# Pipelined evictions in the second network, with its splits, its operands and its conversion moved

## The chip, the cores and the metric

The kernel runs on one core of a Trainium2 chip. The metric is the device time of one execution in microseconds, the median of several runs. TensorE (PE in the rows) does the matrix products, VectorE (DVE), ScalarE (ACT) and GpSimd (POOL) the elementwise work; SyncE (SP) issues the DMAs. Every engine takes its instructions in the order in which the program lists them, and an instruction that waits holds up those behind it on its engine.

## The reference, cut to what matters

```python
attn = softmax over a window of 64 positions of (q @ k.T) / sqrt(64)   # 2 x 8 heads, 576 positions
x = (attn @ v), as 1152 tokens x 512
out = 0
for e in range(4):                      # mixture: w1 512 x 1024, w2 1024 x 512
    h = np.maximum(x @ w1[e], 0.0)
    out += p[:, e:e + 1] * (h @ w2[e])
h = out @ w_in                          # second network: w_in 512 x 2048, w_out 2048 x 512
g = np.maximum(h, 0.0) + alpha * np.minimum(h, 0.0)
return g @ w_out
```

`w_in` and `w_out` arrive as 64-bit floats, everything else as 32-bit floats.

## The kernel before

Attention runs first, interleaved with stage 0 of the mixture. From then on the work goes in stages of 512 hidden columns: stages 1 to 7 are the rest of the mixture, stages 8 to 11 the second network (`S1 = 8`, `NST = 12`). Tokens are in two parts, p = 0 with 512 tokens and p = 1 with 640.

A stage has two phases. Phase A computes the hidden values with one level of a seven-product scheme over 2x2 blocks, which needs sums of blocks of x and w as operands. For each part there are seven units A(s, p, i), i = 0 to 6, and each does one product for u = 0 and one for u = 1, of 256 columns (p = 0) or 320 (p = 1). Products 0, 1 and 2 are copied out of PSUM by ACT (`keep`, L401). Products 3 to 6 end one result each: DVE adds PSUM and the kept copy (`total`, L405; product 6 needs none) and `evict` does the rest. Phase B, nine units B(s, p, t), multiplies the hidden values with w2, and DVE adds each result to `acc` (L523, L527; in stage 8 ACT copies it, L525). A product is done with a high and a low part of each operand, so each operand is split: ACT rounds to the high part, DVE or POOL subtracts to get the low one. The splits are `forms_w1` (L166) for w1 and its block sums, `split_w2` (L210) for w2, `x_first` and `x_second` (L346, L352) for x and its block sums.

In the second network `evict` (L432) has four steps for a result. ACT makes `g` = relu(-src) (L438); DVE makes g = g * alpha + src (L439); `flush(1)` then issues, for the result before this one, ACT's high part `hh` (L484) and POOL's low part `hl` (L485). In the mixture there is one ACT and one DVE instruction for a result.

Between stage 7 and stage 8 the operand x changes: the sums in `acc` are transposed on PE (`x2_unit`, L534), copied by ACT to `raw`, and split. Part 0 of it is split during B(7, 1), part 1 during A(8, 0) and B(8, 0), which run before A(8, 1). B(8, 0) takes its units in the order 2, 3, 0, 1.

The 64-bit weights are converted to 32-bit by integer steps on the device: 32 tiles (`conv_steps`, L228), five steps for a tile: ACT L248 and L249; DVE L251 and L252; DVE L255 and the load of a later tile; DVE L260; DVE L263 with POOL L264 and L265. Then a DMA writes the tile to scratch memory (L267). The tile `ct` has six slots of 512 values in a buffer of 3072: a, two of r, two of y and e; y of tile n + 2 takes the slot that the DMA of tile n reads. `pace` (L691) says how many steps follow each unit: 18 in a mixture stage from stage 2 on (four in A, 14 in B), and in the second network two after each B unit and four in A. `load_w` first issues all steps that its tile still lacks (`convert`, L138).

Other work is given to units by `plan`; a list for each unit is issued after its products. A load of weights is issued after the unit in which the buffer that it takes was used last. PSUM has eight banks, taken in turn.

## Time and profile before

| | us |
|---|---|
| median of 3 runs | 688.3 (687.38 to 689.62) |
| the profiled execution, whole | 687.76 |
| its span, first to last instruction | 685.9 |
| PE busy | 624.6 (91% of the span) |
| DVE busy | 459.9 (67%) |
| ACT busy | 315.0 (46%) |
| POOL busy | 286.0 (42%) |

PE's busy time counts every matmul at the length it had, also where the clock was halved. The share of an engine over the whole span says little here, because the stages differ; the stage boundaries can be read from PE's timeline, where L394 is phase A and L504 phase B.

### The profile page before, as it was taken

The numbers are of one execution on the slowest core, as the hardware profiler recorded it, in microseconds if no ns is written. First come the engines' busy times: TensorE is split into PE (matmuls) and PEld (weight loads), VectorE is DVE, ScalarE is ACT, GpSimd is POOL, SyncE is SP. The second block draws the span as 40 slices with busy tenths as digits, with TensorE's granted clock in tenths as the row PEclk, the third lists the DMA queues.
The fourth block names the chain that finished last, engine by engine and source line by source line (L and its number), as shares of the span: only waits on it lengthen the run. The fifth ranks groups of instructions, "written<-read, shape, count | busy, mean of one in ns | idle before, by whom it ended". The sixth has DMA issues, their size and how long they took to land. (4 is left out here: it accounts for less than half of the span.)

```text
span 685.9 us, 10878 instructions
## 1 busy us (share of the span) xinstructions
PE 624.6 (91%) x4032; PEld 555.0 (81%) x4032; DVE 459.9 (67%) x962; ACT 315.0 (46%) x783; POOL 286.0 (42%) x310
## 2 busy tenths in 40 slices
PE   4799989999999999999999999969798972899898
PEld 3678778989989889899898898858687852888886
DVE  4756659676786877867878666862476588566452
ACT  4555435535426426336155263654465522542640
POOL 4636744053143341450524315444553664464340
PEclk9999999999999999999999999979999995899999
DMA  9742001251241251341322420310041125001012
GB/s 320 257 148 63 2 0 63 96 166 62 92 154 63 93 168 45 129 135 62 138 93 85 151 74 15 123 63 0 1 125 60 62 100 207 16 21 57 1 48 92
DMA packets 31653, 62.59 MB, mean 91 GB/s; under 512 B 2288, under 2 KB 11760, under 8 KB 30576
## 3 DMA queue, kind: packets, MB, share of 16 engines
q1 hardware_dynamic: 31600, 61.90, 26.4%
q8 instruction: 31, 0.51, 0.3%
q14 instruction: 22, 0.18, 0.1%
HBM read 51.14 MB, written 10.75 MB: 90 GB/s over the span
## 5 line engine op out<-in xcount | busy, mean ns | idle before, releaser
L504 PE MATMUL o<-w2l,hh 128*128 128x512 f32 (+1 forms) x400 | 156.9, 392 | 7.1 <-ACT hh L484 7.1
L504 PE MATMUL o<-w2h,hl 128*128 128x512 f32 (+1 forms) x400 | 156.4, 391 | 0.1
L504 PE MATMUL o<-w2h,hh 128*128 128x512 f32 (+1 forms) x400 | 156.1, 390 | 0.0
L264 POOL TENSOR_TENSOR ct<-ct 128x512 f32<-128x512 f32 x32 | 44.9, 1402 | 154.7 <-DVE ct L260 85.5
L504 PEld LDWEIGHTS o<-w2l,hh 128*128 128x128 f32 x400 | 75.9, 190 | 22.7 <-ACT hh L484 7.9
L504 PEld LDWEIGHTS o<-w2h,hl 128*128 128x128 f32 x400 | 75.7, 189 | 16.7 <-POOL hl L485 1.2
L504 PEld LDWEIGHTS o<-w2h,hh 128*128 128x128 f32 x400 | 75.9, 190 | 15.0
L485 POOL TENSOR_TENSOR hl<-g,hh 128x256 fp32r<-128x256 f32 (+1 forms) x64 | 52.9, 833 | 68.0 <-ACT hh L484 67.0
L394 PE MATMUL X<-xth,wfl 128*128 128x256 f32 (+1 forms) x264 | 60.2, 310 | 21.3 <-ACT s L401 12.7
L201 DVE TENSOR_TENSOR w2l<-ws,w2h 128x512 fp32r<-128x512 f32 x48 | 36.2, 753 | 50.2 <-ACT w2h L200 50.0
L394 PEld LDWEIGHTS X<-xth,wfl 128*128 128x128 f32 x264 | 43.3, 195 | 25.7 <-ACT s L401 13.8
L523 DVE SCALAR_TENSOR_TENSOR acc<-o,pn,acc 128x512 f32<-128x512 f32 x63 | 46.6, 745 | 21.7 <-PE o L504 21.6
L188 POOL TENSOR_TENSOR sr<-ws 128x256 f32<-128x256 f32 x42 | 38.3, 911 | 52.4 <-DVE wfl L197 44.7
L394 PE MATMUL X<-xtl,wfh 128*128 128x256 f32 (+1 forms) x264 | 57.7, 301 | 0.0
L394 PE MATMUL X<-xth,wfh 128*128 128x256 f32 (+1 forms) x264 | 57.5, 300 | 0.0
L265 POOL TENSOR_TENSOR ct<-ct 128x512 f32<-128x512 f32 x32 | 42.5, 1328 | 33.1 <-DVE ct L263 31.8
L196 ACT ACTIVATE wfh<-sr 128x1024 fp32r<-128x1024 f32 x22 | 23.3, 1059 | 64.2 <-POOL sr L188 62.0
L248 ACT ACTIVATE ct<-wd 128x512 f32<-128x512 uint32 x32 | 21.3, 666 | 66.9 <-DMA cv<-ct 56.5
L394 PE MATMUL Z<-xth,wfl 128*128 128x320 f32 (+1 forms) x176 | 38.7, 301 | 9.2 <-DVE acc L527 9.2
L394 PEld LDWEIGHTS X<-xtl,wfh 128*128 128x128 f32 x264 | 43.8, 195 | 0.0
L394 PEld LDWEIGHTS X<-xth,wfh 128*128 128x128 f32 x264 | 43.6, 194 | 0.0
L197 DVE TENSOR_TENSOR wfl<-sr,wfh 128x1024 fp32r<-128x1024 f32 x22 | 26.9, 1221 | 21.9 <-ACT wfh L196 21.8
(152 smaller groups left out, 1382.2 us busy)
## 6 DMA issues: line engine op xcount, KB each, us to landing
ws<-in_moe_w_dram SPq DMA_DIRECT2D x16, 1024.0 KB, 5.5
wd<-in_moe_w_in_dram SPq DMA_DIRECT2D x16, 512.0 KB, 3.7
cv<-ct SPq DMA_DIRECT2D x32, 256.0 KB, 2.4
wd<-in_moe_w_out_dram SPq DMA_DIRECT2D x16, 512.0 KB, 3.6
ws<-cv SPq DMA_DIRECT2D x8, 1024.0 KB, 5.0
v<-in_v_dram SPq DMA_DIRECT2D x16, 256.0 KB, 5.7
q<-in_q_dram SPq DMA_DIRECT2D x6, 384.0 KB, 6.8
out_dram<-acc SPq DMA_DIRECT2D x8, 256.0 KB, 2.0
```

The costliest lines, as they stand in the source:

```text
L188: e.tensor_tensor(out=sr[o // 2][:, o % 2], in0=x, in1=y, op=op)
L196: nc.scalar.activation(out=view(hi), in_=src, func=AF.Copy)
L197: nc.vector.tensor_tensor(out=view(lo), in0=src, in1=view(hi).bitcast(F32), op=ALU.subtract)
L201: nc.vector.tensor_tensor(out=lv, in0=src, in1=hv.bitcast(F32), op=ALU.subtract)
L248: nc.scalar.activation(out=y, in_=low, func=AF.Copy, scale=2.0 ** -52)
L264: nc.gpsimd.tensor_tensor(out=y, in0=y, in1=e, op=ALU.mult)
L265: nc.gpsimd.tensor_tensor(out=y, in0=r, in1=y, op=ALU.add)
L394: nc.tensor.matmul(ps, lhsT=w[:, d, :], rhs=x[:, d, :], start=(first and m == 0), stop=(m == 5), skip_group_check=True)
L485: nc.gpsimd.tensor_tensor(out=hl, in0=gg, in1=hh.bitcast(F32), op=ALU.subtract)
L504: nc.tensor.matmul(ps, lhsT=h_t[s, p, f][a][:, t * P:(t + 1) * P], rhs=w_t[2, s, f][b][:, cols], start=(n == 0), stop=(n == 3 * NF - 1))
L523: nc.vector.scalar_tensor_tensor(out=at, in0=ps, scalar=sc, in1=at, op0=ALU.mult, op1=ALU.add)
```

## The change

- Evictions of the second network (s >= 8). `evict` now only issues ACT's relu, into a tile `r`, and puts the result in a queue `heads`. `activate` is called after every product: it issues DVE's L439 step of the results in `heads` but the last one, and ACT's and POOL's `hh` and `hl` for the results in a second queue, `tails`, down to a given number that stay: up to four in stages 9 to 11 (they are issued at the next products 0 and 1, or at the first two B units), up to one in stage 8, none from product 5 on. g overwrites the `total` tile, except for product 6, whose g goes to `r`.
- `split_w2` in the second network: at units (0,0), (0,1), (1,0), (1,1) rather than (0,2), (0,5), (1,1), (1,4); in stage 8 at (0,0) twice, (0,1), (0,2). The load of w2 for the stage after moves with the last of them.
- Changeover operands of part 1: forms 1 and 2 are added on POOL at A(8,0,2) and A(8,0,3), forms 3 and 4 on DVE at B(8,0,2) and B(8,0,3), and all splits (ACT and DVE or POOL) go to B(8,0). Before, adding and splitting stood at A(8,0,2) to B(8,0,1), adding on DVE, low parts on POOL.
- Conversion: `ct` has seven slots, three of them for y; a mixture stage issues 22 steps from stage 2 on (18 in B), stage 8 five, and stages 9 and 10 fewer in B and at i = 1, 2 in A.

```diff
-    xr1 = sb.tile([P, 3072], F32, tag="big", name="xr1")
+    xr1 = sb.tile([P, 3584], F32, tag="big", name="xr1")
...
-            a, r, y, e = [view(ct[:, o]) for o in (0, 1 + n % 2, 3 + n % 2, 5)]
+            a, r, y, e = [view(ct[:, o]) for o in (0, 1 + n % 2, 4 + n % 3, 3)]
...
-            nc.sync.dma_start(out=conv[which, s][:, f, :], in_=ct[:, 3 + n % 2])
+            nc.sync.dma_start(out=conv[which, s][:, f, :], in_=ct[:, 4 + n % 3])
...
-    def x_second(p, raw, f, o, w, add_engine, lo_engine):
+    def x_second(p, raw, f, o, w, add_engine, lo_engine, keep=0):
...
-        nc.scalar.activation(out=hi, in_=src, func=AF.Copy)
-        lo_engine.tensor_tensor(out=lo, in0=src, in1=hi.bitcast(F32), op=ALU.subtract)
+        splits.append((hi, lo, src, lo_engine))
+        while len(splits) > keep:
+            split_next()
...
+    def split_next():
+        if splits:
+            hi, lo, src, e = splits.pop(0)
+            nc.scalar.activation(out=hi, in_=src, func=AF.Copy)
+            e.tensor_tensor(out=lo, in0=src, in1=hi.bitcast(F32), op=ALU.subtract)
...
-            evict(s, p, 2 * u + 1, 0, ps)
+            evict(s, p, 2 * u + 1, 0, ps, True)
             del sets[s, p, u]
-        low_parts(1)
+        if s >= S1:
+            activate(1 if i > 2 else 0, int(i < 5) if s == S1 else (2, 0, 4)[min(i, 2)])
+        else:
+            low_parts(1)
...
-            g = late["mid"].tile([P, HALF[1]], F32, tag="g", bufs=3, name=f"g{s}_{p}_{f}_{half}")[:, 0:HALF[p]]
-            nc.scalar.activation(out=g, in_=src, func=AF.Relu, scale=-1.0)
-            nc.vector.scalar_tensor_tensor(out=g, in0=g, scalar=alph[:, col:col + 1], in1=src,
-                                           op0=ALU.mult, op1=ALU.add)
-            tails.append((hh, hl, g))
-            flush(1)
+            r = late["mid"].tile([P, HALF[1]], F32, tag="r", bufs=3, name=f"r{s}_{p}_{f}_{half}")[:, 0:HALF[p]]
+            nc.scalar.activation(out=r, in_=src, func=AF.Relu, scale=-1.0)
+            heads.append((hh, hl, r, alph[:, col:col + 1], src, r if direct else src))
...
-    def flush(keep):
-        while len(tails) > keep:
-            hh, hl, gg = tails.pop(0)
-            nc.scalar.activation(out=hh, in_=gg, func=AF.Copy)
-            nc.gpsimd.tensor_tensor(out=hl, in0=gg, in1=hh.bitcast(F32), op=ALU.subtract)
+    def activate(keep, later):
+        while len(heads) > keep:
+            hh, hl, r, col, src, g = heads.pop(0)
+            nc.vector.scalar_tensor_tensor(out=g, in0=r, scalar=col, in1=src, op0=ALU.mult, op1=ALU.add)
+            tails.append((hh, hl, g))
+        while len(tails) > later:
+            hh, hl, g = tails.pop(0)
+            nc.scalar.activation(out=hh, in_=g, func=AF.Copy)
+            nc.gpsimd.tensor_tensor(out=hl, in0=g, in1=hh.bitcast(F32), op=ALU.subtract)
...
-            units = [(0, i) for i in range(NF)] if s == S1 else [(0, 2), (0, 5), (1, 1), (1, 4)]
+            units = [(0, 2), (0, 5), (1, 1), (1, 4)] if s < S1 else [(0, 0), (0, 1), (1, 0), (1, 1)]
+            if s == S1:
+                units = [(0, 0), (0, 0), (0, 1), (0, 2)]
...
-        spots = [("A", S1, 0, i) for i in (2, 3, 4, 5, 6)] + [("B", S1, 0, t) for t in (2, 3, 0, 1)]
-        for n, (f, (o, w)) in enumerate((f, x) for f in (1, 2, 3, 0, 4) for x in half[1]):
-            plan(spots[n * len(spots) // 10], lambda f, o, w: x_second(1, raw2(1), f, o, w, nc.vector, nc.gpsimd),
-                 None, f, o, w)
+        for n, (f, add, lo, adds, los) in enumerate((
+                (1, nc.gpsimd, nc.vector, ("A", S1, 0, 2), ("B", S1, 0, 2)),
+                (2, nc.gpsimd, nc.gpsimd, ("A", S1, 0, 3), ("B", S1, 0, 3)),
+                (3, nc.vector, nc.gpsimd, ("B", S1, 0, 2), ("B", S1, 0, 0)),
+                (0, None, nc.vector, ("B", S1, 0, 3), ("B", S1, 0, 0)),
+                (4, nc.vector, nc.gpsimd, ("B", S1, 0, 3), ("B", S1, 0, 1)))):
+            for o, w in half[1]:
+                plan(adds, lambda f, o, w, add, lo: x_second(1, raw2(1), f, o, w, add, lo, 9), None, f, o, w, add, lo)
+                plan(los, split_next, None)
...
-            return int(i < 2) if op == "A" else 1 + (s >= S1 or i % 2 == 0)
+            if op == "A":
+                return int(i < 2 if s < S1 else i in (1, 2))
+            return 1 + (s < S1 or s > S1 and i % 2 == 0)
...
                 if unit[3] == 6:
                     low_parts(0)
+                    activate(0, 0 if unit[1] == S1 else 4)
...
-                if unit[1] >= S1:
-                    flush(0)
+                activate(0, max(0, len(tails) - 2) if unit[2] == 0 else 0)
```

## Rows read from the trace of the kernel before

**Rows 1.** The page: busy tenths and PE's granted clock in 40 slices.
```profile
PE   4799989999999999999999999969798972899898
PEclk9999999999999999999999999979999995899999
```
**Rows 2.** Waits of PE: who <- what; us in total, times, longest.
```profile
PE X L394 <- ACT s L401: 12.7, 4, 8.0
PE Z L394 <- DVE acc L527: 9.2, 2, 6.8
PE o L504 <- ACT hh L484: 7.1, 2, 4.0
PE X L394 <- DVE z L405: 7.0, 8, 3.2
```
**Rows 3.** Busy us by stretch, with count; then PEclk, DMA share, GB/s.
```profile
225.91:250.42 24.51, 24.51 (x110) 20.28 (x109) 21.14 (x32) 7.16 (x13) 8.67 (x8) 1.00 0.46 151
...
391.49:413.88 22.39, 22.39 (x170) 22.39 (x168) 15.32 (x35) 13.03 (x31) 2.77 (x2) 1.00 0.20 60
442.02:461.54 19.52, 13.05 (x96) 12.26 (x93) 12.84 (x24) 12.47 (x30) 6.79 (x8) 0.82 0.29 108
461.54:474.07 12.53, 12.53 (x48) 9.99 (x49) 4.73 (x7) 5.35 (x13) 7.87 (x9) 0.88 0.01 2
...
486.68:506.38 19.70, 15.67 (x62) 12.10 (x61) 12.33 (x18) 11.72 (x23) 13.30 (x15) 0.91 0.09 28
506.38:534.90 28.52, 23.67 (x170) 22.57 (x169) 17.00 (x35) 16.00 (x42) 12.18 (x14) 1.00 0.29 93
...
559.41:607.64 48.23, 28.35 (x170) 26.46 (x168) 31.89 (x57) 20.14 (x49) 21.98 (x22) 0.75 0.28 99
...
632.15:657.98 25.83, 23.41 (x169) 22.52 (x168) 12.77 (x27) 14.64 (x39) 7.77 (x11) 1.00 0.01 1
```
**Rows 4.** Timeline at the start of A(10, 0): PE, then ACT.
```profile
567.78 0.79 PE L394 MATMUL Z<-xth,wfl 128*128 128x256 f32 x2 [6.78 <-DVE acc L527]
...
579.95 0.66 ACT L248 ACTIVATE ct<-wd 128x512 f32<-128x512 uint32 x1 [6.59 <-DMA cv<-ct]
```
**Rows 5.** Timeline of DVE in A(11, 0): one result and the next.
```profile
638.20 0.42 DVE L405 TENSOR_TENSOR s<-W,s 128x256 f32<-128x256 f32 x1
639.16 0.48 DVE L439 SCALAR_TENSOR_TENSOR g<-g,alph,s 128x256 f32<-128x256 f32 x1 [0.55 <-ACT g L438]
639.57 0.42 DVE L405 TENSOR_TENSOR s<-W,s 128x256 f32<-128x256 f32 x1
```
**Rows 6.** Timeline of ACT in A(11): the same results, and a split of w2.
```profile
640.08 0.42 ACT L438 ACTIVATE g<-s 128x256 f32<-128x256 f32 x1 [0.95 <-DVE s L405]
640.40 0.40 ACT L484 ACTIVATE hh<-g 128x256 fp32r<-128x256 f32 x1
...
646.16 0.62 ACT L200 ACTIVATE w2h<-ws 128x512 fp32r<-128x512 f32 x1
```
**Rows 7.** Timeline of A(8, 0): DVE beside POOL.
```profile
455.42 0.89 DVE L439 SCALAR_TENSOR_TENSOR g<-g,alph,z 128x256 f32<-128x256 f32 x1 [0.51 <-ACT g L438]
456.23 0.41 DVE L405 TENSOR_TENSOR z<-X,z 128x256 f32<-128x256 f32 x1
...
455.16 0.87 POOL L366 TENSOR_TENSOR xtl<-tr,xth 128x320 fp32r<-128x320 f32 x1 [1.53 <-ACT xth L365]
```
**Rows 8.** Groups of instructions by form: count, busy us, mean ns, idle before.
```profile
L485 POOL TENSOR_TENSOR hl<-g,hh 128x320 fp32r<-128x320 f32 x32 | 28.0, 887 | 22.1 <-ACT hh L484 21.1 <-PE X L394 0.7
L485 POOL TENSOR_TENSOR hl<-g,hh 128x256 fp32r<-128x256 f32 x32 | 24.9, 779 | 45.9 <-ACT hh L484 45.9
L255 DVE SCALAR_TENSOR_TENSOR ct<-wd,ct 128x512 uint32<-128x512 uint32 x32 | 23.8, 744 | 0.9
...
L260 DVE TENSOR_SCALAR ct<-ct 128x512 uint32<-128x512 uint32 x32 | 14.5, 454 | 1.7 <-DVE ct L255 0.5
```
**Rows 9.** Timeline of DVE where a mixture stage's phase B ends.
```profile
250.62 0.75 DVE L523 SCALAR_TENSOR_TENSOR acc<-o,pn,acc 128x512 f32<-128x512 f32 x1 [1.38 <-PE o L504]
```

More of the change, by code (lines that the diff above doesn't have):

```diff
@@ L215, in big_as @@
     def big_as(name):
-        t = sb.tile([P, 3072], F32, tag="big", name=name)
+        t = sb.tile([P, 3584], F32, tag="big", name=name)
         if name == "ct":
-            late[name] = t.rearrange("p (o m) -> p o m", o=6)
+            late[name] = t.rearrange("p (o m) -> p o m", o=7)
         else:
@@ L364, in x_second @@
             add_engine.tensor_tensor(out=src, in0=x, in1=y, op=ALU.subtract)
-        nc.scalar.activation(out=hi, in_=src, func=AF.Copy)
-        lo_engine.tensor_tensor(out=lo, in0=src, in1=hi.bitcast(F32), op=ALU.subtract)
+        splits.append((hi, lo, src, lo_engine))
+        while len(splits) > keep:
+            split_next()
+    splits = []
+    def split_next():
[3 more added lines that the diff above has]
+            e.tensor_tensor(out=lo, in0=src, in1=hi.bitcast(F32), op=ALU.subtract)
     def tr_tile(p, i, o, raw):
@@ L430, in h_tiles, with evict @@
         return h_t[s, p, f]
-    def evict(s, p, f, half, src):
+    def evict(s, p, f, half, src, direct=False):
         c = slice(half * HALF[p], (half + 1) * HALF[p])
@@ L478, in tile_kernel @@
     hc_t, h_c = {}, {}
-    tails = []
-    def flush(keep):
-        while len(tails) > keep:
-            hh, hl, gg = tails.pop(0)
-            nc.scalar.activation(out=hh, in_=gg, func=AF.Copy)
-            nc.gpsimd.tensor_tensor(out=hl, in0=gg, in1=hh.bitcast(F32), op=ALU.subtract)
+    heads, tails = [], []
+    def activate(keep, later):
[7 more added lines that the diff above has]
+            nc.gpsimd.tensor_tensor(out=hl, in0=g, in1=hh.bitcast(F32), op=ALU.subtract)
     def l2_chunk(c, t):
```

## The prediction

> **What bounds the kernel now.** I read the page first. PE's tenths stand at nine from the fourth slice on, and fall only in the last third, where the granted clock falls with them [rows 1]. So PE is the bound, and the question is what it waits for in that last third. The view of PE's waits answers with four lines: kept copies by ACT, `acc` by DVE, `hh` by ACT, totals by DVE, 36.0 us in all [rows 2]. None of them is a transfer. What a wait costs together with the clock is seen best in the table by stretch [rows 3]. An undisturbed phase A takes 22.39 us and an undisturbed phase B 24.51, with PE busy throughout; the columns of the parts being 256 and 320, phase A divides into 9.95 and 12.44, or 0.71 and 0.89 us for a product. Against these, the second network loses:
> - A(8, 0) and B(8, 0): 19.52 + 12.53 = 32.05 us, where 9.95 + 4/9 x 24.51 = 20.84 would do. Two transposes, eight instructions, lie in the stretch and stay; at 22.39/168 = 0.13 us each that is 1.0, so 10.2 are lost.
> - B(8, 1): 19.70 against 5/9 x 24.51 = 13.62, 6.1 lost.
> - A(9): 28.52 - 22.39 = 6.1. A(10): 48.23 - 22.39 = 25.8. A(11): 25.83 - 22.39 = 3.4.
>
> Together 51.6 us, all that this change can win; the mixture stages have nothing to give.
>
> **Conversion.** A(10) is the largest term. Counting steps through `pace` and `convert`: before, 108 of the 160 steps are issued by the end of the mixture's pace, and when the w1 load of stage 11 is issued, at B(9,0,2), it finds 26 tiles done and 28 needed, so 11 steps (2.2 tiles) are issued at one go. ACT then sits behind L248, which waits 6.59 us for the DMA of the tile two before, and `acc` is late on DVE behind the same steps, so PE waits 6.78 us for a bank [rows 4]; the clock of the stretch is 0.75 [rows 3]. After, 132 steps are issued by the same point, the three stages' loads find 27, 28 and 29 tiles where 20, 24 and 28 are needed, and no step is forced; y has a third slot. The cause is gone whole. A(11) has no conversion at all, and shows what stays once the burst is gone: 3.4 us. So the conversion part is worth 25.8 - 3.4 = 22.4 in A(10), and part of A(9), whose ACT queue also has steps in it.
>
> Its price lies in the mixture. Four steps more in a phase B are 0.8 tile. A tile is 3.15 us of DVE (the five groups from L255, 744 ns, to L260, 454 ns [rows 8]), so DVE gets 2.5 us more. The fullest phase B has DVE at 21.14 of 24.51 us [rows 3], so it would be at 23.7: it still fits, and DVE waits 1.38 us for PE at that phase's end [rows 9]. What spills over lands in phase A, where PE needs DVE for the first time after product 3, so after 6 x 0.71 = 4.3 us. ACT is at 7.16 and POOL at 8.67 of 24.51 there, far from full. I put the price at 0.1 us for each of six stages, 0.6, between 0 and 3 (0.5 each, should a spill outlast the cover).
>
> **Evictions.** In A(11) one result takes DVE from 638.20 to 639.57, 1.37 us, for two instructions that fill 0.83 of it; the 0.55 between them is the wait for ACT's relu [rows 5]. Results come from PE every 0.71 us. Over eight results DVE falls 8 x (1.37 - 0.71) = 5.3 us behind, and the kept copies of part 1 stand on ACT behind relus and `hh` that wait for DVE: that is the wait of X for s, which after its longest one, 8.0, leaves (12.7 - 8.0)/3 = 1.6 us for each of three stages [rows 2]. After the change, DVE does the total of result n + 1 while ACT does the relu of n: 0.37 + 0.41 = 0.78 us a result (its pitches on either side of the wait in [rows 5]), and product 6 has no total. Eight results take 6 x 0.37 + 8 x 0.41 = 5.5 us, against 5.7 on PE. DVE keeps up. ACT has 0.42 for the relu and 0.40 for `hh` [rows 6], of which four are put off to the next products 0 and 1, where ACT has only 0.4 a product for kept copies. The w2 splits (0.62 on ACT [rows 6], some 0.7 on DVE) move from the middle of this into products 0 and 1, beside copies that leave both engines room.
>
> New waits: the kept copy of part 1 writes a buffer whose g the late `hl` still reads, so ACT can wait for POOL. Four `hl` at 0.78 us [rows 8] follow product 5 one by one and are needed about 0.9 us apart; behind that ACT instruction stand the other copies, and PE needs the first of them only two units later. Cover enough; without it the loss would be up to 1 us a part. I leave 0.3 us of A(11), 0.8 of A(9) and 0.8 of A(10), which still carry four or five steps; so they gain 3.1, 5.3 and 25.0, **33.4 together**. Bounds: 35.3 (nothing left) and 28 (2.5 us left in each).
>
> One row speaks against this. With POOL at work on SBUF, L439 took 0.89 us, ending 0.28 after POOL's instruction, while L405, which reads one operand from PSUM, took its usual 0.41 beside POOL [rows 7]. So L439 and an `hl` exclude each other; before, they took turns by themselves, since `hl` starts when L439 has ended. The Trainium skill says so too, in SBUF — State Buffer, Who interferes with whom: a VectorE instruction with two inputs in SBUF and a GpSimd instruction that reads SBUF take the shared port in turns, each for its whole length. By that rule each result would take 0.41 + 0.78 = 1.19 us rather than 0.78; the row bears it out, and it is the first rival. In stages 9 to 11 it bites little, as only four of eight `hl` come up while L439s are left.
>
> **The changeover.** B(8, 1) waits for the last results: PE had `hh` 4.0 us late at the most [rows 2], and then half the clock. With the chain cut, the last result of DVE comes some 3 us earlier; but in stage 8 all eight `hl` of 0.89 us [rows 8] come at once, 7.1 us, as long as PE takes for the eight products. Starting after the second result, so some 3 us into them, they end 3 us after PE does, or 5 if four L439s of 0.5 us take turns with them, and PE has 0.7 us of work before it needs the seventh. I take **3.0** of the 6.1 (bounds 1 and 5.5). In A(8, 0) the additions of forms 1 and 2 leave DVE's queue, and with them ACT's splits that waited for them; but four additions on POOL (0.87 each by the nearest row of that size, a subtraction [rows 7]) fall on the low parts of w2 and x on DVE and exclude them by the same row, 3.5 us. The first total comes hardly earlier than now; behind it the results flow at 0.78 to 1.2 instead of 1.37 with splits between. Their splits fall into B(8, 0), 11 us of PE with DVE busy 4.73 and ACT 5.35 [rows 3]: six low parts on POOL (5.3 us), four additions and four low parts on DVE (some 4 us) fit, and the last is not needed before product 6 of A(8, 1). I take **3.0** of 10.2, between -2 (the additions on POOL hold DVE's w2 parts and all that follows) and 6.5.
>
> **Sum.** 33.4 + 3.0 + 3.0 - 0.6 = 38.8 us. The profiled execution took 687.76 (span 685.9 and 1.9 around it), which gives 649.0; it lies 0.5 below the median of the runs, so 649.5. Best bounds: 35.3 + 5.5 + 6.5 = 47, 641. Worst, all at once: 28 + 1 - 2 - 3 = 24, 664.
>
> **Rivals.**
> 1. The port takes the place of the wait. L439 and `hl` take turns throughout, 1.19 us a result in part 0 and 0.51 (0.41 for 320 columns) + 0.89 = 1.40 in part 1, against 0.71 and 0.89 from PE. For: [rows 7]. Against: only half of the `hl` are issued in the stretch. Then 1.5 us stay in each of A(9) to A(11), 4.5 instead of 1.9, and the changeover gains nothing, 6.0 less: 649.5 + 2.6 + 6.0, about 658.
> 2. A mild spill in the mixture: 1.6 us, the wait for a kept copy above, twice in each of six stages, 19 us: about 669. Against: such phases had steps of all five kinds at their first units before, and PE did not wait in one of them [rows 2].
> 3. Slower than before: DVE cannot hold the added steps in the mixture, is more than 4.3 us behind when a phase A begins, and ACT's copies and relus stop behind conversion steps as in A(10). There, 2.2 tiles too many cost 25.8 us with the clock, 11.7 a tile; 24 steps, 4.8 tiles, are moved, 56 us: about 706. Against: 3.4 us free in the fullest phase B [rows 3], and the third slot of y.
> 4. The change does not do what it says: the count is off and steps are still forced at B(9,0,2). The margin is one tile. Then A(10) keeps 22.4: about 672.
>
> **Chances.** The forecast 0.72, rivals 1 to 4 0.14, 0.07, 0.04 and 0.03. The range goes from 641 to 664: it takes in the bounds of the unknown terms and rival 1, and leaves out rivals 2 to 4 and a little at both ends. All but rival 3 are faster by far more than 0.3% (2 us, about what a measurement of this kernel can tell from no change): faster 0.95, same 0.01, slower 0.04.
>
> **What would show it.** Right: A(9), A(10) and A(11) at 22.4 to 23.5 us each with the clock at 1.00; no wait of ACT L248 over 1 us beside them; DVE's L405 and L439 in turn without idle time between; mixture stages at 46.9 us as before; B(8, 1) at about 16.7 us. Wrong: L439 at 0.8 to 0.9 us in most places and X waiting for totals (rival 1); waits of PE before 413 us (rivals 2 and 3); two cv writes close together at B(9, 0) with ACT idle between (rival 4). What I trust least is stage 8, where POOL, DVE and ACT all change places at once.

## The result, and the profile after

The changed kernel takes 655.95 us (median of four executions, 655.19 to 657.06) where the kernel before, beside it, takes 688.87 (687.38 to 689.62; the 688.3 read before is the median of three of these four). The ratio is 0.9526, with a 95% interval of 0.9503 to 0.9549. The forecast was 649.5, in a range of 641 to 664. The sign and the size of the largest term came as forecast; 6.4 us of the gain are missing, and two places account for most of that, the mixture's phases A and B(9, 1).

The profiled execution took 655.72 us, with a span of 653.9, against 687.76 and 685.9 before: 32.0 us to be found. First the page's slices, PE's busy tenths and the granted clock, to be held against [rows 1]:

```profile
PE   4899998999999899999999999999799998999998
PEclk8699998999999999999999999999899998999999
```

The hole of the last third (a 2 among sevens and eights, with the clock at 5) is gone. What is left are a 7, which is B(8, 0), and single eights. The view of PE's waits (who <- what; us in total, times, longest) has no entry above 4 us that belongs to the two networks; before, four lines held 36.0 [rows 2]:

```profile
PE o L517 <- POOL hl L498: 4.0, 3, 1.8
PE o L517 <- ACT hh L497: 3.9, 3, 1.6
PE X L403 <- DVE z L414: 3.6, 3, 2.2
```

L517 is phase B's matmul (L504 before), L403 phase A's (L394), L414 the total (L405), L493 the multiply-add (L439), L497 and L498 `hh` and `hl` (L484, L485).

Then the table by stretch. Columns as in [rows 3]: stretch and its length, then busy us and count of PE, PE's weight load, DVE, ACT and POOL, then PE's granted clock, DMA share and GB/s. The stretches are A(3, 0), A(8, 0), B(8, 0), B(8, 1), A(9), B(9, 1), A(10) and A(11):

```profile
204.49:217.16 12.67, 10.47 (x86) 10.17 (x84) 12.32 (x20) 5.48 (x14) 7.93 (x8) 1.00 0.36 120
447.90:460.34 12.44, 11.43 (x95) 11.02 (x93) 10.10 (x17) 9.10 (x22) 5.40 (x6) 1.00 0.40 148
460.34:475.66 15.32, 12.74 (x48) 10.10 (x49) 6.87 (x14) 7.89 (x21) 8.52 (x11) 0.89 0.05 19
487.98:504.76 16.78, 14.22 (x62) 11.11 (x61) 9.66 (x13) 9.36 (x18) 10.81 (x14) 1.00 0.00 0
504.76:527.16 22.40, 22.40 (x170) 22.39 (x169) 15.77 (x34) 15.40 (x40) 9.28 (x10) 1.00 0.39 136
538.05:556.37 18.32, 15.54 (x61) 12.10 (x60) 14.76 (x21) 6.61 (x12) 9.73 (x11) 0.91 0.31 115
556.37:578.75 22.38, 22.38 (x169) 22.38 (x168) 18.75 (x37) 14.30 (x38) 12.18 (x12) 1.00 0.20 72
603.66:626.06 22.40, 22.40 (x170) 22.39 (x169) 14.85 (x31) 14.99 (x40) 6.51 (x8) 1.00 0.01 2
```

Phase A of stages 9, 10 and 11 is now PE busy from end to end at full clock. Still longer than PE needs are A(3, 0) (10.07 would do), B(8, 0) (10.90), B(8, 1) and B(9, 1) (13.61 each), and in A(8, 0) 1.0 us of idle time is left. In A(3, 0) DVE is busy for 12.32 of 12.67 us.

With the boundaries set by PE's instructions in both traces, the account of the span is:

| stretch | before | after | gain | forecast |
|---|---|---|---|---|
| A(9) + A(10) + A(11) | 102.57 | 67.17 | 35.4 | 33.4 |
| B(8, 1) | 19.70 | 16.78 | 2.9 | 3.0 |
| A(8, 0), B(8, 0), A(8, 1) | 44.67 | 40.08 | 4.6 | 3.0 |
| part 0 of A(2) to A(6) | 50.74 | 55.17 | -4.4 | -0.6, with the next row |
| B(7, 0) | 12.15 | 12.95 | -0.8 | |
| B(9, 1) and B(10, 1) | 27.22 | 32.32 | -5.1 | 0 |
| start to the end of A(1) | | | -0.6 | 0 |
| sum | | | 32.0 | 38.8 |

(PE's wait at a boundary counts to the phase that follows.)

**Evictions.** DVE in A(11, 0), start and duration, beside [rows 5]:

```profile
610.35 0.41 DVE L414 TENSOR_TENSOR z<-X,z 128x256 f32<-128x256 f32 x1
610.68 0.47 DVE L493 SCALAR_TENSOR_TENSOR s<-r,alph,s 128x256 f32<-128x256 f32 x1
611.07 0.42 DVE L414 TENSOR_TENSOR z<-X,z 128x256 f32<-128x256 f32 x1
611.41 0.47 DVE L493 SCALAR_TENSOR_TENSOR z<-r,alph,z 128x256 f32<-128x256 f32 x1
```

Total and multiply-add follow each other with no idle time between, 0.73 us a result (610.68 to 611.41) where it was 1.37; PE delivers one every 0.71.

**What is new in B(9, 1).** ACT (four lines), then PE (two), then POOL, in brackets the idle time before and what ended it:

```profile
537.28 1.06 ACT L196 ACTIVATE wfh<-sr 128x1024 fp32r<-128x1024 f32 x1 [5.47 <-POOL sr L188]
538.24 0.66 ACT L248 ACTIVATE ct<-wd 128x512 f32<-128x512 uint32 x1
538.80 0.65 ACT L249 ACTIVATE ct<-wd 128x512 f32<-128x512 f32 x1
539.36 0.81 ACT L497 ACTIVATE hh<-r 128x320 fp32r<-128x320 f32 x2
539.87 0.50 PE L517 MATMUL o<-w2l,hh 128*128 128x512 f32 x1 [0.97 <-ACT hh L497]
542.41 0.80 PE L517 MATMUL o<-w2h,hl 128*128 128x512 f32 x1 [1.81 <-POOL hl L498]
541.31 2.05 POOL L498 TENSOR_TENSOR hl<-r,hh 128x320 fp32r<-128x320 f32 x2
```

The last two tails of part 1 are issued at B(9, 0, 1). By then ACT's queue holds the split of stage 10's weight forms, which waits 5.47 us for POOL's sums, and two conversion instructions. PE stands at the first product of B(9, 1) while `hh`, whose input was long ready, is behind them; `hl` follows on POOL, and PE waits again. Of the 4.7 us that B(9, 1) loses, 2.8 are this idle time (18.32 - 15.54) and 1.9 the clock, 0.91 in the stretch.

**What is new in A(3, 0).** DVE (four lines), POOL (two), PE:

```profile
209.43 1.53 DVE L251 TENSOR_SCALAR ct<-ct 128x512 f32<-128x512 f32 x1
210.99 1.40 DVE L252 TENSOR_SCALAR ct<-ct 128x512 uint32<-128x512 uint32 x1
212.31 1.22 DVE L201 TENSOR_TENSOR w2l<-ws,w2h 128x512 fp32r<-128x512 f32 x1
213.46 0.74 DVE L414 TENSOR_TENSOR s<-W,s 128x256 f32<-128x256 f32 x2
209.20 1.47 POOL L264 TENSOR_TENSOR ct<-ct 128x512 f32<-128x512 f32 x1 [2.67 <-DVE ct L260]
210.75 1.36 POOL L265 TENSOR_TENSOR ct<-ct 128x512 f32<-128x512 f32 x1
215.47 0.51 PE L403 MATMUL X<-xth,wfl 128*128 128x256 f32 x2 [2.20 <-DVE z L414]
```

The phase began at 204.49 and its first total comes at 213.46, 9 us later. Ahead of it on DVE stand conversion instructions that end 0.3 us after POOL's of the same time: L251 ends at 210.96 with L264 at 210.67, L252 at 212.39 with L265 at 212.11. PE runs out of banks and waits 2.20 us.

### The profile page after: what moved, and what is told of

Same layout as the page of the kernel before. It is cut to its first block, busy times and chain, and to the rows that moved or that the text cites. A ratio compares the mean times of both kernels' runs of the same rounds, so it can differ in the third digit from the quotient of the medians.

```text
span 653.9 us, 10946 instructions
## 1 busy us (share of the span) xinstructions
PE 620.6 (95%) x4032; PEld 552.9 (85%) x4032; DVE 470.3 (72%) x962; ACT 313.6 (48%) x783; POOL 287.1 (44%) x310
## 4 chain that ended last, share of the span: by engine, by line
PE 64%; DVE 15%; ACT 8%; POOL 8%; issue 4%; DMA 1%; SPq 0%; DVEq 0%; POOLq 0%; ACTq 0%
PE o L517 29%; PE X L403 15%; PE Z L403 7%; PE W L403 4%; POOL hl L498 3%; PE h L472 2%; PE oc L505 2%; POOL sr L188 2%; ACT wfh L196 2%; DVE wfl L197 2%; DVE acc L536 1%; DMA ws<-in_moe_w_dram 1%; DVE w2l L201 1%; PE pv L329 1%; DVE ct L251 1%
## 5 line engine op out<-in xcount | busy, mean ns | idle before, releaser
L517 PE MATMUL o<-w2h,hl 128*128 128x512 f32 (+1 forms) x400 | 156.8, 392 | 4.1 <-POOL hl L498 4.0
L517 PE MATMUL o<-w2l,hh 128*128 128x512 f32 (+1 forms) x400 | 156.8, 392 | 3.9 <-ACT hh L497 3.9
L517 PE MATMUL o<-w2h,hh 128*128 128x512 f32 (+1 forms) x400 | 155.9, 390 | 0.0
L264 POOL TENSOR_TENSOR ct<-ct 128x512 f32<-128x512 f32 x32 | 44.5, 1390 | 150.6 <-DVE ct L260 79.3
L517 PEld LDWEIGHTS o<-w2h,hl 128*128 128x128 f32 x400 | 75.9, 190 | 21.5 <-POOL hl L498 5.9
L517 PEld LDWEIGHTS o<-w2l,hh 128*128 128x128 f32 x400 | 75.9, 190 | 19.8 <-ACT hh L497 4.9
L517 PEld LDWEIGHTS o<-w2h,hh 128*128 128x128 f32 x400 | 75.7, 189 | 14.9
L201 DVE TENSOR_TENSOR w2l<-ws,w2h 128x512 fp32r<-128x512 f32 x48 | 38.8, 812 | 38.7 <-ACT w2h L200 37.7
L403 PE MATMUL X<-xth,wfl 128*128 128x256 f32 (+1 forms) x264 | 57.8, 300 | 3.9 <-DVE z L414 3.6
L265 POOL TENSOR_TENSOR ct<-ct 128x512 f32<-128x512 f32 x32 | 43.5, 1359 | 31.5 <-DVE ct L263 30.1
L403 PE MATMUL X<-xth,wfh 128*128 128x256 f32 (+1 forms) x264 | 56.6, 295 | 0.0
L403 PE MATMUL X<-xtl,wfh 128*128 128x256 f32 (+1 forms) x264 | 56.6, 295 | 0.0
L188 POOL TENSOR_TENSOR sr<-ws 128x256 f32<-128x256 f32 x42 | 36.2, 862 | 38.6 <-DVE wfl L197 30.7
L403 PEld LDWEIGHTS X<-xth,wfl 128*128 128x128 f32 x264 | 42.5, 189 | 5.5 <-DVE z L414 4.4
L403 PEld LDWEIGHTS X<-xth,wfh 128*128 128x128 f32 x264 | 42.6, 190 | 0.0
L403 PEld LDWEIGHTS X<-xtl,wfh 128*128 128x128 f32 x264 | 42.6, 189 | 0.0
L298 ACT ACTIVATE p<-sm,st 128x128 f32<-128x128 f32 x72 | 28.0, 390 | 27.0 <-DVE st L295 27.0
L197 DVE TENSOR_TENSOR wfl<-ws,wfh 128x512 fp32r<-128x512 f32 (+1 forms) x44 | 35.7, 851 | 6.9 <-ACT wfh L196 6.9
```

Of the source, the lines that this page charges most:

```text
L188: e.tensor_tensor(out=sr[o // 2][:, o % 2], in0=x, in1=y, op=op)
L197: nc.vector.tensor_tensor(out=view(lo), in0=src, in1=view(hi).bitcast(F32), op=ALU.subtract)
L201: nc.vector.tensor_tensor(out=lv, in0=src, in1=hv.bitcast(F32), op=ALU.subtract)
L264: nc.gpsimd.tensor_tensor(out=y, in0=y, in1=e, op=ALU.mult)
L265: nc.gpsimd.tensor_tensor(out=y, in0=r, in1=y, op=ALU.add)
L298: nc.scalar.activation(out=pt[:, hp, :], in_=sm[:, hp, :], func=AF.Exp, scale=-1.0, bias=st[:, 0, hp:hp + 1], accum_out=st[:, 1, hp:hp + 1])
```

## Experiments

Each kernel below computes the whole result. Each differs from the changed kernel ("after") by the edit shown, unless it says otherwise; lines that only follow from an edit, or that it takes out, are left out where "..." stands. A kernel is called by the short name given where its edit stands (e2, e8 and so on); ratios are to the kernel before, with their 95% interval.

### The conversion's share

```
             if op == "A":
-                return int(i < 2 if s < S1 else i in (1, 2))
-            return 1 + (s < S1 or s > S1 and i % 2 == 0)
+            return int(i < 2) if op == "A" else 1 + (s >= S1 or i % 2 == 0)
```

The pace of before, all else as after (e2):

> The changed kernel with the old pace of the conversion in all stages; the third slot of y and all else stay. Theory (forced steps are the largest term): 11 steps are issued at one go at B(9, 0, 2) again and A(10, 0) loses some 22 us, while the mixture's phases A(2, 0) to A(6, 0) return to 10.1 us each and give back 4.4: about 673. Rival (the evictions and the third slot do it): with ACT and DVE freed the burst drains beside PE, A(10, 0) stays within 3 us of 10.1, and the time is 651 to 655.

Measured: 671.73 us (669.13 to 673.32), 0.9745 [0.9714, 0.9777], near the theory's 673. A(10, 0) has the burst back, and the mixture's loss is gone. The stretches A(3, 0) and A(10, 0), columns as above, and ACT in the burst:

```profile
204.34:214.40 10.06, 10.06 (x85) 10.06 (x84) 8.06 (x18) 5.05 (x13) 2.69 (x3) 1.00 0.36 127
554.85:580.37 25.52, 13.07 (x86) 12.37 (x84) 23.31 (x38) 9.01 (x20) 11.97 (x9) 0.73 0.46 163
569.97 0.67 ACT L248 ACTIVATE ct<-wd 128x512 f32<-128x512 uint32 x1 [7.79 <-DMA wd<-in_moe_w_out_dram]
```

A(10) takes 40.1 us instead of 22.4, 17.7 more, and part 0 of A(2) to A(6) gets back its 4.4. B(8, 1), which has ten conversion steps here and five in after, takes 2.75 more with the same waits of PE as in after (1.3 us for `hh`, 1.3 for `hl`), at a lower clock; the last section comes back to it. So at the new evictions the pace is worth 17.7 in A(10). The third y slot alone doesn't help the burst: ACT's wait has gone from the tile's own DMA [rows 4] to the load of the next tile, 7.79 us.

The opposite, the conversion's part alone: the kernel before with the new pace and the seven slots of `ct` (e8).

```
(against the kernel before)
-            return int(i < 2) if op == "A" else 1 + (s >= S1 or i % 2 == 0)
+            if op == "A":
+                return int(i < 2 if s < S1 else i in (1, 2))
+            return 1 + (s < S1 or s > S1 and i % 2 == 0)
...
-            a, r, y, e = [view(ct[:, o]) for o in (0, 1 + n % 2, 3 + n % 2, 5)]
+            a, r, y, e = [view(ct[:, o]) for o in (0, 1 + n % 2, 4 + n % 3, 3)]
...
```

> The kernel before with the change's conversion alone: pace, 22 steps in a mixture stage, and ct of seven slots. Theory (the burst is a cost by itself, 22.4 us by the forecast, and the mixture gives 4.4 back): A(10) falls to about A(11)'s 25.8, 688.5 - 22.4 + 4.4 = 670.5. Rival (with the old evictions, A(9) and A(10) stay long whatever the conversion does): 676 or more.

Measured: 675.9 us (674.51 to 678.24), 0.9809 [0.9787, 0.9831], between the two and just under the rival's 676. The stretch A(10):

```profile
564.15:595.09 30.94, 25.60 (x170) 24.71 (x169) 21.96 (x40) 15.54 (x41) 14.84 (x16) 0.89 0.17 70
```

A(10) falls from 48.2 to 30.9, by 17.3, and not to the 25.8 that A(11) takes without any conversion. With the evictions in lockstep, 8.5 us are still lost there. Do the two parts need each other? By the profiled spans conversion alone gains 12.6 (685.9 to 673.3) and all but the pace 14.6 (685.9 to 671.3), 27.2 of the 32.0 that both gain. Of the 4.8 that are over, 2.75 are the clock of B(8, 1) in the one, and 1.4 that of A(3) in the other (last section); 0.6 is left. So in these executions the parts add up, if the clock's share is taken out.

### The evictions' share

After with the eviction of before (relu and multiply-add in lockstep on one result, low parts at once; e3). The core of the edit:

```
-            heads.append((hh, hl, r, alph[:, col:col + 1], src, r if direct else src))
+            nc.vector.scalar_tensor_tensor(out=g, in0=g, scalar=alph[:, col:col + 1], in1=src,
+                                           op0=ALU.mult, op1=ALU.add)
+            tails.append((hh, hl, g))
+            activate(0, 1)
...
```

> The changed kernel with the old evictions (relu, multiply-add, and the high and low part of the result before, in one go), all else as changed. Theory (the lockstep of ACT and DVE is what A(11) showed): A(9), A(10) and A(11) take about 26 us each instead of 22.4, 10.5 in all; A(8, 0) with B(8, 0) and B(8, 1) lose about 6; B(9, 1) and B(10, 1) give back 5, since no result is put off: about 667. Rival (moving the splits of w2 and the conversion is enough): A(9) to A(11) stay below 23 us, and the time is 651 to 658.

Measured: 667.19 us (666.38 to 668.04), 0.9683 [0.9666, 0.9701], as the theory said. Stretches A(9), A(10), A(11):

```profile
510.06:535.83 25.77, 23.71 (x170) 22.52 (x169) 14.25 (x31) 16.42 (x42) 10.14 (x13) 1.00 0.34 133
560.34:588.90 28.56, 24.87 (x170) 24.07 (x168) 20.02 (x40) 15.80 (x41) 13.44 (x16) 0.94 0.23 91
613.42:637.78 24.36, 23.15 (x170) 22.45 (x168) 13.23 (x27) 14.80 (x39) 7.70 (x11) 1.00 0.01 2
```

They lose 3.4, 6.2 and 2.0 us, 11.5 together, and B(8, 1) 3.0 (19.74 against 16.78), half of it in PE's wait (4.0 us once instead of 1.3 twice), the rest by the clock (0.91 instead of 1.00). A(8, 0), B(8, 0) and A(8, 1) together lose 1.2 (41.3 against 40.1). B(9, 1) and B(10, 1) take 13.61 each, the 5.1 us being back: with the old eviction no tail is left for unit 1 of phase B. So the new eviction is worth 14 to 16, by whether the clock of B(8, 1) is counted, and costs 5.1 as it is written.

### The tails that stay behind

```
             elif op == "B":
-                activate(0, max(0, len(tails) - 2) if unit[2] == 0 else 0)
+                activate(0, 0)
```

All tails are issued before B's first unit, ahead of the weight forms of the next stage (e1):

> The changed kernel, but all results still in tails are issued at the first B unit, where the changed kernel leaves two of them for the second. Theory (order on ACT and POOL): B(9, 1) stalls because the last two hh stand on ACT behind forms_w1 of stage 10, which waits 5.5 us for POOL, and behind a conversion step; issued ahead of these they are ready long before B(9, 1). B(9, 1) goes from 18.3 to 13.6 us and B(10, 1) from 14.0 to 13.6, so 655.9 to about 651. Rival (POOL's work itself): POOL has the same low parts and block sums to do either way, and the wait moves to a later place: no better than 655.

Measured: 657.8 us (656.73 to 660.53), 0.956 [0.9533, 0.9587], against 0.9526 [0.9503, 0.9549] for after: nothing is won. Stretches B(9, 1) and A(10, 0) of this kernel, and DVE's first multiply-add of A(10, 0) in it; last the same instruction in after:

```profile
537.78:551.39 13.61, 13.61 (x62) 11.26 (x60) 9.83 (x13) 5.32 (x8) 8.39 (x9) 1.00 0.11 26
551.39:566.87 15.48, 11.40 (x86) 10.79 (x85) 15.10 (x29) 6.09 (x15) 7.06 (x6) 0.96 0.37 148
563.08 0.59 DVE L493 SCALAR_TENSOR_TENSOR s<-r,alph,s 128x256 f32<-128x256 f32 x1 [0.15 <-ACT r L450]
```
```profile
563.17 0.62 DVE L493 SCALAR_TENSOR_TENSOR s<-r,alph,s 128x256 f32<-128x256 f32 x1 [0.15 <-ACT r L450]
```

The wait in B(9, 1) is gone whole (13.61), and A(10) gets it all back: A(10, 0) takes 15.48 instead of 10.07, and A(10, 1) 1.0 more as well. DVE's first multiply-add comes at the same time in both, 563.08 and 563.17. So the tails were not what ends last. What the two traces point to is a chain that goes through POOL's sums, ACT's split, DVE's low part and the conversion: it sets when DVE reaches A(10)'s results, and after merely pays for it earlier, in B(9, 1).

If so, the chain must get shorter, and POOL's sums are its head. The edit above, with the sums for the second network's later stages given to DVE (e7):

```
-        e = nc.vector if (s, u) == (1, 0) else nc.gpsimd
+        e = nc.vector if (s, u) == (1, 0) or s > S1 else nc.gpsimd
```

> The kernel of e1_flush_all, and the block sums of w1 for stages 9 to 11 on DVE instead of POOL. Theory (a chain through POOL, ACT and DVE sets the end of stage 9's phase B): in e1_flush_all and in the changed kernel the conversion steps of B(9) end at the same time, whatever PE waited for, because ACT sits 5 to 6 us before the rounding of the block sums, which POOL reaches only after eight low parts; without POOL in that chain its steps come 5 us earlier, B(9, 1) takes 13.6 us and A(10) 22.4 to 23.4: 650.5 to 652. Rival (DVE itself is full in stage 9): the four sums, 1.7 us a block and more in turns with the low parts on POOL, delay DVE by as much as POOL did; A(10) or B(9, 1) keep 3 us or more: 654 to 658.

Measured: 655.18 us (652.83 to 657.42), 0.9519 [0.9482, 0.9556]. ACT's split and DVE's first multiply-add, then the stretch A(10, 0):

```profile
534.94 1.06 ACT L196 ACTIVATE wfh<-sr 128x1024 fp32r<-128x1024 f32 x1 [2.03 <-DVE sr L188]
560.59 0.62 DVE L493 SCALAR_TENSOR_TENSOR s<-r,alph,s 128x256 f32<-128x256 f32 x1 [0.15 <-ACT r L450]
552.04:563.84 11.80, 10.59 (x86) 10.18 (x85) 11.45 (x22) 5.38 (x14) 5.73 (x4) 1.00 0.21 81
```

The chain ends 2.5 us earlier than in e1, A(10, 0) takes 11.8 and B(9, 1) 13.61. So in the trace the theory's chain is shown, and of the 5.1 us in B(9, 1) and B(10, 1) 3.4 are won; 1.7 stay in A(10, 0), more than the theory allowed, and that execution took 652.83. The median lies in the rival's range, because two of the four executions took 657.3 and 657.4. They have no trace; their mean granted clock was 0.977 and 0.982, against 0.990 in the two short ones. What could lengthen them by as much is seen in B(8, 1) and in A(3) (last section), but that is argued, not shown.

### The mixture's price

The same 22 steps in a stage, but the four of phase A all in part 1, where DVE has more room (9.0 busy of 12.3 us in A(3, 1) of after), and none in part 0 (e9):

```
-                return int(i < 2 if s < S1 else i in (1, 2))
+                return 2 * p * int(i < 2) if s < S1 else int(i in (1, 2))
```

> The changed kernel; in the mixture the steps that stood at A(s, 0, 0) and A(s, 0, 1) go to A(s, 1, 0) and A(s, 1, 1), two at each, still 22 in a stage. Theory (DVE enters phase A behind, and the steps there, in turns with POOL, make product 3's total late): A(2, 0), A(3, 0), A(5, 0) and A(6, 0) go back to 10.1 us, 4.4 less: about 651.5. Rival (too many steps in a stage, wherever they are): phase A(s, 1) loses what A(s, 0) gains, or A(s, 0) stays long: 654 to 658.

Measured: 651.86 us (651.25 to 652.5), 0.9471 [0.9455, 0.9488], faster than after. Stretches A(3, 0) and B(8, 0):

```profile
204.07:214.63 10.56, 10.47 (x85) 10.17 (x84) 10.09 (x18) 4.41 (x11) 7.31 (x7) 1.00 0.44 148
457.15:471.04 13.89, 11.31 (x50) 9.04 (x49) 6.88 (x14) 7.90 (x21) 8.55 (x11) 1.00 0.07 27
```

A(3, 0) gains 2.1, A(5, 0) 1.4 and A(2, 0) 0.4, A(6, 0) loses 0.4: 3.5 us. So it is not the number of steps in a stage that costs, but what of it stands ahead of the first totals. The two steps of units 0 and 1 stood there before too, and cost hardly anything; with the four added to phase B, more of B's steps come late and run into A. In A(3, 0) DVE had four conversion instructions ahead of its first total before (2.7 us), seven in after (6.0 us) and five here (3.1 us), and the total came 6.2, 9.0 and 7.0 us into the phase. Another 1.4 us are no work of the edit: B(8, 0) has the same idle time of PE in both (13.89 - 11.31 and 15.32 - 12.74, 2.58 each) and its clock is 1.00 here, 0.89 in after.

Does the third y slot matter, now that nothing bursts? After with two (e4):

```
-            a, r, y, e = [view(ct[:, o]) for o in (0, 1 + n % 2, 4 + n % 3, 3)]
+            a, r, y, e = [view(ct[:, o]) for o in (0, 1 + n % 2, 3 + n % 2, 5)]
...
```

> The changed kernel with ct of six slots, two for y as before; all else as changed. Theory (22 steps a stage leave time for the DMA): ACT waits more in its first conversion instruction, in phases where nobody needs it; 655 to 658. Rival (the third slot is what lets the mixture take 22 steps): ACT is held ahead of kept copies and relus in the mixture's phases A, which lose 1 us or more each: 662 or more.

Measured: 658.96 us (657.55 to 660.66), 0.9565 [0.9542, 0.9587], 3.0 more than after and between the two expectations. ACT waits for the tile's own DMA again, twice in A(5, 0):

```profile
302.52 0.68 ACT L248 ACTIVATE ct<-wd 128x512 f32<-128x512 uint32 x1 [5.38 <-DMA cv<-ct]
308.13 0.67 ACT L248 ACTIVATE ct<-wd 128x512 f32<-128x512 uint32 x1 [2.77 <-DMA cv<-ct]
```

A(5, 0) takes 13.08 (11.45 in after) and A(6, 0) 11.73 (10.54). The slot earns its place by the pace of the mixture, not by stage 10.

### The changeover's parts

Three edits, one for each part that moves in stage 8. First the operands of part 1 issued as before, two halves of a form at each unit, additions on DVE (e5):

```
+        spots = [("A", S1, 0, i) for i in (2, 3, 4, 5, 6)] + [("B", S1, 0, t) for t in (2, 3, 0, 1)]
+        for n, (f, (o, w)) in enumerate((f, x) for f in (1, 2, 3, 0, 4) for x in half[1]):
+            plan(spots[n * len(spots) // 10], lambda f, o, w: x_second(1, raw2(1), f, o, w, nc.vector, nc.gpsimd),
+                 None, f, o, w)
...
```

> The changed kernel with the changeover's operands of part 1 planned as before: added on DVE and split at once, from A(8, 0, 2) to B(8, 0, 1). Theory (adds and splits in the middle of the results hold ACT and DVE): A(8, 0) and B(8, 0), 27.8 us in the changed kernel, lose 2 to 4 of the 4.3 gained: 658 to 660. Rival (the additions on POOL cost DVE in turns what they save): within 1 us, 655 to 657, or faster.

Measured: 661.82 us (658.56 to 661.99), 0.9601 [0.957, 0.9632]. A(8, 0) and B(8, 0):

```profile
448.26:461.34 13.08, 11.46 (x95) 11.05 (x93) 10.15 (x19) 10.02 (x24) 3.39 (x4) 1.00 0.44 160
461.34:479.26 17.92, 13.96 (x50) 10.81 (x50) 7.58 (x12) 7.65 (x19) 11.95 (x14) 0.81 0.01 1
```

31.0 us against 27.8, so the move is worth 3.2 in these executions: 2.0 are idle time of PE, 1.2 the clock of B(8, 0), 0.81 against 0.89. The profiled execution is 6.1 us over that of after; the rest lies where the edit changes nothing: 1.5 in A(3), 1.4 in B(8, 1) and 1.4 in B(9, 1), each at a lower clock, less 1.5 at the start and in small terms.

Second, the splits of w2 at the units of before (e6):

```
-            units = [(0, 2), (0, 5), (1, 1), (1, 4)] if s < S1 else [(0, 0), (0, 1), (1, 0), (1, 1)]
-            if s == S1:
-                units = [(0, 0), (0, 0), (0, 1), (0, 2)]
+            units = [(0, i) for i in range(NF)] if s == S1 else [(0, 2), (0, 5), (1, 1), (1, 4)]
```

> The changed kernel with the splits of w2 at their old units. Theory (each is 0.6 us of ACT and 0.7 of DVE in the middle of the results, where the pipelined chain has hardly any slack): A(9) to A(11) lose about 0.7 us each and A(8, 0) 1: about 659. Rival (the pipelined chain takes them in its stride): within 1 us of the changed kernel, 655 to 657.

Measured: 662.71 us (661.21 to 663.25), 0.9625 [0.9606, 0.9644]. A(8, 0) loses 0.9, A(9) 1.2, A(10) 0.5, B(9, 1) 2.0 (its clock at 0.83) and B(10, 1) 1.2: 5.8 us, and 1.5 more in A(3), which the edit leaves alone. A(11) loses nothing, where the theory had 0.7. Splits between the results make the results late, and most of it is paid in phase B: in B(9, 1) PE waits 2.5 us for `hh` and 1.3 for `hl`, 3.8 against 2.8 in after, and the lower clock adds the rest.

Third, only the additions of forms 1 and 2 back on DVE (e13):

```
-                (1, nc.gpsimd, nc.vector, ("A", S1, 0, 2), ("B", S1, 0, 2)),
-                (2, nc.gpsimd, nc.gpsimd, ("A", S1, 0, 3), ("B", S1, 0, 3)),
+                (1, nc.vector, nc.vector, ("A", S1, 0, 2), ("B", S1, 0, 2)),
+                (2, nc.vector, nc.gpsimd, ("A", S1, 0, 3), ("B", S1, 0, 3)),
```

> The changed kernel, but the additions of forms 1 and 2 at A(8, 0, 2) and A(8, 0, 3) on DVE, splits in B(8, 0) as changed. The forecast held that these four additions on POOL cost DVE in turns nearly what they save. If so (first theory) the time is within 1 us of the changed kernel, 655 to 657. Rival (POOL had the time, and DVE had not): totals and multiply-adds of A(8, 0) come later by four additions of 0.4 to 0.5 us, PE waits up to 2 us more at A(8, 0) or B(8, 0): 657 to 659.

Measured: 658.37 us (656.48 to 661.17), 0.9554 [0.953, 0.9578]. A(8, 0) takes 12.76 (12.44 in after) and B(8, 0) 15.33 (15.32), so by the trace POOL's additions are worth 0.3 us, as the first theory has it. The two sides of the exchange can be read too: in after, a low part of w2 and one of x on DVE take 1.37 and 1.50 us beside POOL's additions, and 0.69 and 0.82 here; the four additions on DVE take some 1.8 here. The median, 2.4 above after, lies in the rival's range; the profiled execution, 656.48, is 0.8 above, and holds 1.4 more in A(3), shown below. What makes the other executions longer is open.

### All repairs together

Three of the edits above in one kernel (all tails at once, sums on DVE, the mixture's steps in part 1; e10):

> The changed kernel with the edits of e7_sums_dve and e9_mix_p1 together. Theory (two separate places, stage 9's chain and the mixture's phases A(s, 0)): the gains add. In the profiles e9 saved some 3.3 in the mixture, e7 4.7 + 0.4 in B(9, 1) and B(10, 1) less 1.7 that it left in A(10, 0): 655.95 - 3.3 - 3.4, about 649. Rival (what is won early is lost in stage 9, whose chain sets its own end, as in e1_flush_all): not below e9's 651.9.

Measured: 649.95 us (648.04 to 652.06), 0.9424 [0.94, 0.9447]: the gains add, as the theory said. And with two steps more in part 1 of each mixture stage, 24 in place of 22, so that stages 9 and 10 convert less (e12; against after, with the other two edits as they are):

```
-                return int(i < 2 if s < S1 else i in (1, 2))
+                return 2 * p * int(i < 3) if s < S1 else int(i in (1, 2))
```

> The kernel of e10_all, with two steps more at A(s, 1, 2) of each mixture stage, 24 in a stage, so that the conversion ends in B(9) and A(10) has none. Theory (what is left in A(10, 0) is conversion that reaches into it): A(10, 0) goes from 11.8 us in e7_sums_dve to 10.1, and the mixture still holds 24 steps, since they stand where only part 1's results wait: 647 to 648. Rival (the mixture is full at 22): A(s, 1) or A(s + 1, 0) lose 0.5 us or more in each stage: 650 or more.

Measured: 649.38 us (648.77 to 650.15), 0.9421 [0.9408, 0.9434]: the same time as with 22. A(10, 0) now takes 10.07 as its theory said (11.83 with 22) and B(7, 0) 0.8 less, but A(2) to A(7) give 3.9 us back, as the rival had it. These two are the fastest kernels of the study, 1.0% under after and 5.8% under before.

## Why the prediction was right, and where it failed

**The total** came into its range with errors of both signs: losses of 10.3 us that the sum did not have stand against 3.5 us of gains beyond it, and that they met so well is partly luck. By the number alone, 655.95 is nearer to the first rival's 658 than to 649.5. The stretches tell them apart: that rival kept 4.5 us in A(9) to A(11), where nothing is left, and gave the changeover nothing, which gained 7.5.

**The burst and the lockstep** were the right diagnosis. A(9) to A(11) gained 35.4 us against the 33.4 forecast; the 1.9 us that were left for conversion steps inside the stages did not stay, since PE runs all three at 22.4. How the sum is shared between the parts was mis-sized. "The conversion part is worth 22.4" supposed that A(10) without the burst would look like A(11); it looks like 30.9 (e8), so conversion alone is worth 17.3, and 17.7 at the new evictions (e2). The lockstep is worth 11.5 (e3) in the three stages at the new pace. Steps without a burst, merely in the queues, go with a longer phase where the eviction goes back and forth between ACT and DVE: A(10) is 5.1 us longer than A(11) in e8 and 4.2 in e3, and as long as A(11) in after.

**The eviction's pitch**, 0.78 forecast, is 0.73; the rows that the forecast cites give 0.82 (1.37 - 0.55), so part of the 0.78 was a misreading to the good side. The first rival, L493 and `hl` taking turns, is there in places: the first two multiply-adds of A(10, 0) take 0.62 and 1.18 in place of 0.47, and six of the sixteen of stage 8 take 0.61 to 1.17. No stretch of A(9) to A(11) is longer for it.

**The changeover.** 3.0 and 3.0 were forecast, with bounds far apart; 2.9 and 4.6 came, the first by half for another reason: in B(8, 1) PE's idle time fell from 4.0 to 2.6 us, by 1.5 and not 3, and the other half is the clock, 0.91 before and 1.00 in this execution. That 2.9 met 3.0 is luck. Of the parts, the operands' move is worth 3.2, w2's move 0.9 in A(8, 0) (with more in the stages after), and the additions on POOL 0.3. So the lower bound's mechanism, that POOL's additions hold up DVE's low parts, is there (1.37 us in place of 0.69, see e13), but it costs no more than the additions would on DVE, and the hope that the move relieves DVE came to little.

**The mixture's price** is the term that failed: 0.6 with an upper bound of 3, and 4.4 measured, 5.2 with B(7, 0). The step that failed is the cover. It set DVE's 23.7 us against the 24.51 of a phase B, and 4.3 us more until PE needs a total. The 4.3 were not too many: before, the first total of A(3, 0) came 6.2 us into the phase and PE did not wait. But DVE falls further behind than a phase's sum says. The steps of a tile do not spread themselves evenly; two of them are issued at units 0 and 1 of phase A itself, ahead of the totals, and behind whatever has piled up at the end of phase B, and the first total came after 9.0 us. And a tile's 3.15 us is a mean: L252 took 0.43 alone and 1.40 beside POOL's L265. The second rival, a mild spill, was the nearest in kind, at a quarter of its price, though PE waited for DVE's totals and not for kept copies. It had seen the steps at the first units, and took it for a sign of safety that PE had not waited for them. e9 shows the place: the same number of steps, none in part 0, and 3.5 of the 4.4 are back.

The rule of the Trainium skill that the prediction weighed (SBUF — State Buffer, Who interferes with whom) says more than the prediction took from it: not only an instruction with two SBUF inputs takes the port that GpSimd uses; `tensor_scalar` can too, in the mode that uses both ports. L251 and L252 are `tensor_scalar` instructions on SBUF, and the trace agrees: 1.53 and 1.40 us, each until 0.3 us after POOL's end. The prediction applied the rule to the eviction, where it decides nothing in stages 9 to 11, and not to the conversion, where the turns cost DVE some 2 us in A(3, 0) (1.53 + 1.40, against 0.43 each). How much of PE's 2.20 us wait is theirs, and how much the added steps', is not shown: no kernel here takes POOL's part of the conversion away.

**A wait that was not foreseen**, 5.1 us: the last two tails behind stage 10's weight forms. "New waits" asked what the late `hl` would hold up, and not what would hold up the late `hh`. The instruction ahead of it waits for another engine, 5.47 us, and such rows were in the trace of before (the same split, 3.69 and 5.21 us for POOL's sums in B(9)), where nothing stood behind them that PE needed in B(9). But e1 shows that this wait is not the cause of the loss, only the place of it: issuing the tails earlier puts the same loss into A(10). The bound is the chain from POOL's sums, and it couldn't be seen before, while A(10) lost 25.8 us. e7 shortens it, and 3.4 of the 5.1 us are back; in e12, with no conversion left in A(10, 0), all of it is.

The third and the fourth rival fell: no conversion step is forced at B(9, 0), and the mixture keeps up but for the waits above.

The missing 6.8 us of the account: 4.6 in the mixture and B(7, 0), 5.1 in B(9, 1) and B(10, 1), 0.6 at the start, less 2.0 and 1.5 that the stages and the changeover gave over the forecast. The 0.6 at the start lies ahead of all that the change touches, and the clock there differs between executions.

## What to carry to other kernels

When an eviction goes to and fro between two engines, its pitch is the sum of both and their handshakes; let one engine work on the next result meanwhile, and the pitch falls to the busier engine's own work (1.37 to 0.73 us here). Work that is put off must be looked at in the queue it is put into: what stands ahead of it there, and on whom does that wait? And work that is moved into "free" time must be costed at the units where it is issued, with durations taken from beside the engine that will be running there, for a share of a whole phase hides the first microseconds, in which the next phase needs the engine.
